# New priorities for the same tasks: one core, attention by hash buckets and two gated layers in one list schedule

## The chip, the cores and the metric

The kernel runs on one core of one Trainium2 chip. The metric is the device time of one execution in microseconds. The time before is 852.47 us, the median of three runs (852.0 to 852.72).

## What is computed

Three stages in float32, each feeding the next. First an attention over 2 batches of 8 heads, 768 rows of 64: six sign bits of `q @ proj` and `k @ proj` give each row a bucket, and a row attends only to rows of its own bucket. Then a gated layer on 1536 tokens, and then a second layer. The weights come as float64, in words of 64 bits.

```python
mask = q_bucket[:, :, :, None] == k_bucket[:, :, None, :]
scores = np.where(mask, scale * q @ k.T, -1e9)
attn = softmax(scores) @ v                      # 2 x 8 x 768 x 64
x = attn as 1536 x 512
xn = x / sqrt(mean(x * x) + 1e-6) * rms_g
x = (silu(xn @ w_gate) * (xn @ w_val)) @ w_out  # 512 -> 1536 -> 512
h = x @ w2_in                                   # 512 -> 2048
out = where(h > 0, h, exp(min(h, 0)) - 1) @ w2_out
```

## The kernel before

Each float32 factor is kept as two float32r parts, a rounded one (`hi`) and the remainder (`lo`), and a product is the sum of three matmuls. So nearly every tile that TensorE (PE) reads has been made by one copy on ScalarE (ACT), which rounds, and one subtraction on VectorE (DVE) or GpSimd (POOL), which forms the remainder.

The attention goes by 8 pairs of heads, and a pair by 6 units of 256 query rows. A unit is: scores of two blocks of 128 rows (`ps_s`, L477), their maximum on DVE (`nm`, L484), the exponential on ACT (`p`, L494), three turns of 4 transposes (`ps_p`, L522), the two parts of each turned tile (`pt`: ACT copy L530 and DVE subtraction L534; for some units the first turn goes through an ACT copy `pf`, L539, and two POOL instructions, L543 and L546), and three weighings of the values (`ps_v`, L569), which DVE joins into `ot` (L587). Beside the units the next pair is prepared: doubled rows `rd` on POOL, transposes `ps_t`, operands `tq` and `tk`, sign bits `ps_b` and counts `ps_c`. After a pair, its sums are inverted (`r`, L605 and L610), widened on POOL (`rw`, L618), transposed (`ps_x`, L627) and multiplied into `xT` (L636). After four pairs one batch is normalised: squares `sq`, `ps_z`, then multiplications (L731, L732) and a subtraction `xn` (L746), on POOL for the first batch and on DVE for the second.

The two layers go by 5 and 6 groups of hidden blocks of 128. A group's weights arrive in halves (`wraw`), and each half is converted: ACT L811, DVE L814, L820, L827 and L834 build float32 words from 64 bits (`wf`), ACT L855 rounds (`whi`), POOL L859 subtracts (`wlo`). A hidden block is `ps_h` (L908) on PE, then `sg`, `hf` and the two parts of `h` (L933 to L958); `ps_y` (L993) and `ps_o` (L1048) sum over a group, and DVE adds the sum up (L1005, L1060). The first group's blocks on the first batch begin while the last pair's attention still runs.

No engine's order is written out. Every task is handed to a planner (class `Plan`) with its engine, an assumed length, what it reads and writes, its buffers and a priority. The planner plays the program through: at each step it takes, over all engines, the task that can start first, and among tasks of one engine that could start at the same time the one with the smaller priority number. The instructions are then issued in that order, and on the chip each engine keeps to it and waits by semaphores.

A priority is a place in the natural order of units plus an offset from the table `OFF`, by kind of task and head pair: `S` scores, `max`, `exp`, `T` turns, `hi` and `lo` (and `plo` on POOL) the parts of `pt`, `V` weighings, `my` joins, `prep` and `post`, `norm` and `norm0` the normalisations, `ld` loads, `pv` values, `w0` and `w0s` the first group's weight loads, `wc` the conversions.

```python
fits.append(((t, prio), i))
plan.add("DVE", dve(S), top, [B_], [N_], prio + off("max", j))
prio += OFF["wc"]
```

Of the kernel before, what the change touches and what calls it, by code (L numbers as in the profile page):

```python
# [29 lines left out]
BYPOOL = ([0, 1, 2, 3, 4], [0, 2, 3, 4], [0, 1, 2, 3, 4, 5], [2, 4], [2, 4], [2, 4], [2, 4], [0])  # L30
HOT = ('DVE', 'ACT', 'ACT', 'DVE')
BW = (384, 512)
OFF = {'S': [-0.746, -0.843, -1.864, 66.85, -0.744, -0.758, -0.224, -0.41], 'max': [86.06, 128.957, 190.513, 53.124, 102.143, -5.035, -10.834, 24.749], 'exp': [119.567, 67.059, 76.291, 2.774, 75.069, 56.662, -35.846, 43.868], 'T': [0.573, 0.48, 0.307, 0.831, 0.703, 1.127, 1.259, 1.321], 'hi': [36.303, -33.663, 1.961, -57.136, 22.322, 57.959, -91.469, -121.974], 'lo': [-34.121, 9.653, 32.465, -109.77, -12.636, -87.223, -67.192, -11.818], 'V': [2.027, 1.953, 1.894, 2.015, 1.865, 2.222, 2.417, -11.303], 'my': [76.979, -114.216, -55.16, -8.134, -134.423, -45.978, -63.486, -29.752], 'ld': [16.116, 103.645, 134.666, -130.684, 51.199, 277.906, -45.786, 44.455], 'pv': [19.903, -68.605, 49.828, -156.296, 63.827, 116.499, -168.838, 19.653], 'prep': [-0.809, -2.78, -3.346, -0.341, -0.21, -0.194, 0.226, -82.459], 'post': [4.851, 4.774, 2.643, 1.592, 3.332, 9.244, 3.712, 28.29], 'plo': [-227.264, -10.728, 0.013, -54.307, -64.379, -36.39, 74.399, -48.961], 'wc': 0.693, 'ld1': 50.459, 'norm0': -125.474, 'rush': 27.318, 'pstep': 0.316, 'qstep': 0.146, 'norm': -8.853, 'w0': 189.461, 'w0s': 3.7229545865993564e+29}


class Plan:
# [143 lines left out]
def kernel(  # L180
# [69 lines left out]
    def off(key, j):  # L250
        return OFF[key][j]

# [12 lines left out]
    def dma(fn, nbytes, r=(), w=(), prio=None):  # L265
        return plan.add("SP", max(0.57, nbytes / 360e3), fn, r, w, prio, 2.7)
# [3 lines left out]
    def load_qk(j, prio, gate=()):  # L270
        b, h0 = divmod(2 * j, H)

        def go(i, a):
            if ("raw", j) not in st:
                st["raw", j] = slot([128, 2, 2, NC, D], F32, "raw")
            nc.sync.dma_start(
                out=st["raw", j][:, i, a], in_=(q, k)[i][b, h0 + a].rearrange("(p c) d -> p c d", c=NC)
            )

        for a in range(2):  # L280
            for i in range(2):
                dma(
                    lambda i=i, a=a: go(i, a), S * D * 4, r=[("go", j - 2), *gate],
                    w=[(("slot", "raw", j), i, a)], prio=prio + 0.05 * a,
                )
# [12 lines left out]
    def prep_v(j, prio):  # L298
        def hi(a):
            if ("vv", j) not in st:  # L300
                st["vv", j] = slot([128, 2, NC, 128], F32R, "vv")
            nc.gpsimd.tensor_copy(
                out=st["vv", j][:, a, :, 64 * a:64 * a + 64], in_=st["vn", j][:, a]
            )

        def lo(a):
            vv = st["vv", j]
            nc.gpsimd.tensor_tensor(
                out=vv[:, a, :, 64 - 64 * a:128 - 64 * a], in0=st["vn", j][:, a],
                in1=f(vv[:, a, :, 64 * a:64 * a + 64]), op=ALU.subtract,  # L310
            )

        for a in range(2):
            plan.add("Pool", 1.4, lambda a=a: hi(a), [("h3", "vn", j)], [(("slot", "vv", j), a, 0)], prio)
            plan.add(
                "Pool", 1.0, lambda a=a: lo(a),
                [("h3", "vn", j), (("slot", "vv", j), a, 0)], [(("slot", "vv", j), a, 1)], prio,
            )
# [124 lines left out]
    def prep(j, prio, step):  # L443
        p = prio
        for a in range(2):
            for i in range(2):
                twice(j, a, i, p)
                for hf in range(2):
                    prep_T(j, a, i, hf, p)
                    p += step  # L450
        for hf in range(2):
            prep_bits(j, hf, p)
            p += step
        for i in range(2):
            for hf in range(2):
                prep_count(j, i, hf, p)
                p += step
# [321 lines left out]
    def weights(g, m, part, prio, gate):  # L779
# [19 lines left out]
        dma(load, 128 * cols * (8 if wide else 4), r=gate, w=[R_], prio=prio)  # L799
        prio += OFF["wc"]  # L800
        if wide:
# [370 lines left out]
    prep_v(0, -15)  # L1172
    load_qk(1, OFF["ld1"])

    UPP = NC
    NU = NPAIR * UPP
    for j in range(NPAIR):
# [14 lines left out]
        if j + 1 < NPAIR:  # L1192
            prep(j + 1, base + off("prep", j), OFF["pstep"])
        hurry = OFF["rush"] if j == NPAIR - 1 else 0.0
        post(j, base + UPP + off("post", j) - hurry, OFF["qstep"])
        if j % PPB == PPB - 1:
# [70 lines left out]
```

## Time and profile before

| | us |
|---|---|
| median of three runs | 852.47 |
| the profiled execution | 852.93 |
| its span, first to last instruction | 851.1 |
| PE busy | 832.4 (98%) |
| DVE busy | 638.5 (75%) |
| ACT busy | 444.9 (52%) |
| POOL busy | 273.3 (32%) |

The profile is one execution. Busy time is the time in which an engine has at least one instruction in work; PE's matmuls overlap each other, so a busy PE is not PE at its peak. The shares are means over the whole span, and the stages differ: the attention fills roughly the first 290 us, the layers the rest. A wait in the lists is idle time of an engine together with the instruction whose end released it.

### The profile page before, as it was taken

Reading aid. Unit: us, or ns where it says so; the run is one execution under the profiler, and the core shown is the slowest. Engines: PE = TensorE matmul, PEld = TensorE weight load, DVE = VectorE, ACT = ScalarE, POOL = GpSimd, SP = SyncE. Lnnn points to the kernel's source line nnn. Section 1 sums busy time; section 2 is a strip of 40 time slices with the busy share of each in tenths; the row PEclk is TensorE's granted clock in tenths of the full one; section 3 lists DMA queues with packets and bytes.
Section 4 is the critical chain, followed back from the end, with each engine's and each line's share of the span. In section 5 each row is a group of like instructions: output and inputs, shape, how many; then the busy total and the mean of one; then the engine's idle time right before and its main releaser. Section 6 shows DMA issues by size and latency. Waiting matters only on the chain.

```text
span 851.1 us, 12464 instructions
## 1 busy us (share of the span) xinstructions
PE 832.4 (98%) x4722; PEld 736.7 (87%) x4722; DVE 638.5 (75%) x1015; ACT 444.9 (52%) x838; POOL 273.3 (32%) x289
## 2 busy tenths in 40 slices
PE   8999999998999999999999999999999999999998
PEld 7999999887998899999889898887888888888786
DVE  6999899999999987534364565579857778676754
ACT  6988988898987664432222322235444333332321
POOL 7857476789824312111011111110201101111100
PEclk9999999999999999999999999999999999999999
DMA  5102012330002200310111312213121302001003
GB/s 168 41 17 75 2 38 75 121 122 1 20 1 75 75 13 26 112 50 1 56 48 46 100 50 100 75 33 128 62 75 37 112 25 75 25 30 46 1 12 137
DMA packets 25708, 49.05 MB, mean 58 GB/s; under 512 B 2480, under 2 KB 8880, under 8 KB 25648
## 3 DMA queue, kind: packets, MB, share of 16 engines
q1 hardware_dynamic: 25648, 48.25, 17.3%
q8 instruction: 37, 0.61, 0.3%
q14 instruction: 23, 0.19, 0.1%
HBM read 45.09 MB, written 3.15 MB: 57 GB/s over the span
## 4 chain that ended last, share of the span: by engine, by line
PE 81%; DVE 13%; ACT 4%; issue 1%; POOL 1%; ACTq 0%; DVEq 0%; POOLq 0%
PE ps_h L908 37%; PE ps_o L1048 14%; PE ps_y L993 11%; PE ps_p L522 5%; PE ps_v L569 5%; PE ps_s L477 4%; DVE nm L484 3%; DVE pt L534 3%; PE ps_t L350 2%; PE ps_b L398 2%; ACT p L494 1%; ACT pt L530 1%; DVE wf L827 1%; DVE wf L834 1%; PE ps_w L1153 1%
## 5 line engine op out<-in xcount | busy, mean ns | idle before, releaser
L859 POOL TENSOR_TENSOR wlo<-wf,whi 128x768 fp32r<-128x768 f32 (+1 forms) x54 | 86.8, 1607 | 442.9 <-ACT whi L855 430.6
L908 PE MATMUL ps_h<-xn,whi 128*128 128x512 f32 (+2 forms) x768 | 190.2, 337 | 0.8 <-DVE hf L939 0.7
L908 PEld LDWEIGHTS ps_h<-xn,whi 128*128 128x128 f32 x768 | 133.5, 189 | 13.2 <-DVE hf L939 1.1
L908 PE MATMUL ps_h<-xn,wlo 128*128 128x256 f32 (+2 forms) x384 | 128.9, 336 | 0.0
L1048 PE MATMUL ps_o<-whi,h 128*128 128x512 f32 (+1 forms) x388 | 118.7, 387 | 0.8 <-DVE oa L1060 0.8
L908 PE MATMUL ps_h<-y,whi 128*128 128x512 f32 x384 | 118.2, 389 | 0.0
L933 ACT ACTIVATE sg<-ps_h 128x512 f32<-128x512 f32 (+1 forms) x87 | 50.7, 583 | 116.6 <-PE ps_h L908 114.5
L855 ACT CAST whi<-wf 128x768 fp32r<-128x768 f32 (+1 forms) x54 | 39.6, 733 | 118.2 <-DVE wf L834 118.2
L569 PE MATMUL ps_v<-pt,vv 128*128 128x256 f32 x576 | 96.8, 295 | 4.1 <-DVE pt L534 3.2
L954 ACT CAST h<-hf 128x512 fp32r<-128x512 f32 (+1 forms) x87 | 51.6, 605 | 88.1 <-DVE hf L939 49.1
L993 PE MATMUL ps_y<-h,whi 128*128 128x512 f32 (+1 forms) x312 | 91.4, 374 | 1.5 <-DVE ya L1005 1.5
L484 DVE TENSOR_REDUCE nm<-ps_s 128x1 f32<-128x768 f32 x96 | 90.6, 945 | 1.6 <-PE ps_s L477 0.9
L958 DVE TENSOR_TENSOR h<-hf,h 128x512 fp32r<-128x512 f32 (+1 forms) x87 | 71.0, 831 | 26.9 <-ACT h L954 26.2
L494 ACT ACTIVATE p<-ps_s,nm 128x768 f32<-128x768 f32 x96 | 87.2, 909 | 5.5 <-DVE nm L484 4.4
L522 PE MATMUL ps_p<-ident,p 128*128 128x128 f32 x576 | 86.0, 275 | 3.3 <-DVE pt L534 1.5
L477 PE MATMUL ps_s<-tk,tq 128*128 128x384 f32 x384 | 87.9, 350 | 0.6 <-ACT tk L428 0.4
L1048 PEld LDWEIGHTS ps_o<-whi,h 128*128 128x128 f32 x388 | 72.2, 188 | 16.4 <-DVE oa L1060 1.9
L569 PEld LDWEIGHTS ps_v<-pt,vv 128*128 128x128 f32 x576 | 79.3, 189 | 7.2 <-DVE pt L534 5.1
L908 PEld LDWEIGHTS ps_h<-y,whi 128*128 128x128 f32 x384 | 72.1, 188 | 15.0
L939 DVE TENSOR_TENSOR hf<-ps_h,sg 128x512 f32<-128x512 f32 (+1 forms) x39 | 25.2, 647 | 78.5 <-PE ps_h L908 78.5
L534 DVE TENSOR_TENSOR pt<-ps_p,pt 128x512 fp32r<-128x512 f32 x120 | 79.9, 680 | 2.7 <-ACT pt L530 1.8
L908 PEld LDWEIGHTS ps_h<-xn,wlo 128*128 128x128 f32 x384 | 72.6, 189 | 5.5
(111 smaller groups left out, 1501.0 us busy)
## 6 DMA issues: line engine op xcount, KB each, us to landing
wraw<-in_moe_w_out_dram SPq DMA_DIRECT2D x12, 768.0 KB, 4.9
wraw<-in_moe_w_in_dram SPq DMA_DIRECT2D x8, 768.0 KB, 4.6
wraw<-in_moe_w_out_dram SPq DMA_DIRECT2D x10, 512.0 KB, 4.1
raw<-in_q_dram SPq DMA_DIRECT2D x16, 192.0 KB, 3.4
raw<-in_k_dram SPq DMA_DIRECT2D x16, 192.0 KB, 3.7
vn<-in_v_dram SPq DMA_DIRECT2D x8, 384.0 KB, 3.3
wraw<-in_moe_w_gate_dram SPq DMA_DIRECT2D x4, 768.0 KB, 4.4
wraw<-in_moe_w_val_dram SPq DMA_DIRECT2D x4, 768.0 KB, 4.6
```

The costliest lines, as they stand in the source:

```text
L477: nc.tensor.matmul(st[B_][:, hf, 0:HS], lhsT=tq[:, x, c * 128:(c + 1) * 128], rhs=tk[:, x, hf * HS:(hf + 1) * HS], start=(x == 0), stop=(x ...
L484: nc.vector.tensor_reduce(out=st["nm", u, cc], in_=st[B_][:, :, 0:HS], axis=AX.XY, op=ALU.max, negate=True,)
L494: nc.scalar.activation(out=halves(st["p", u][:, cc]), in_=st.pop(B_)[:, :, 0:HS], func=AF.Exp, bias=st["nm", u, cc], scale=1.0, accum_out= ...
L522: nc.tensor.transpose(out=st[B_][:, o:o + 128], in_=p[:, cc, (2 * n + kt) * 128:(2 * n + kt + 1) * 128], identity=ident,)
L534: nc.vector.tensor_tensor(out=pt[:, 1], in0=st.pop(B_), in1=f(pt[:, 0]), op=ALU.subtract)
L569: nc.tensor.matmul(st[B_][:, 0:256], lhsT=st["vv", j][:, a, 2 * n + kt, :], rhs=pt[:, x, kt * 256:(kt + 1) * 256], start=(n == seq[0] and ...
L859: nc.gpsimd.tensor_tensor(out=l, in0=s["w"], in1=f(h), op=ALU.subtract)
L908: nc.tensor.matmul(ps[:, o:o + ln], lhsT=w[wp][:, kk, ft * 128:(ft + 1) * 128], rhs=t[xp][:, s:s + ln], start=(kk == 0 and n == 0), stop=( ...
L954: nc.scalar.copy(out=st["h", g, blk, ft][:, 0, 0:bw], in_=s["hf"])
L958: nc.vector.tensor_tensor(out=h[:, 1, 0:bw], in0=s["hf"], in1=f(h[:, 0, 0:bw]), op=ALU.subtract)
L993: nc.tensor.matmul(s["ps"][:, 0:bw], lhsT=wo[wp][:, ft, m * 128:(m + 1) * 128], rhs=h[:, xp, 0:bw], start=(ft == 0 and i == 0), stop=(ft = ...
L1048: nc.tensor.matmul(s["ps"], lhsT=h[:, xp, t * 128:(t + 1) * 128], rhs=wo[wp][:, ft, ds], start=(ft == 0 and i == 0), stop=(ft == n - 1 and ...
```

## The change

One line is replaced, the table `OFF`: all of its offsets but one (`pstep`) get new values. They were searched in a replay of the tasks in which every task carries the delay that was recorded for it on the chip. Tasks, engines, lengths, buffers and pools are as before. A part of the table's line, wrapped:

```diff
-OFF = {'S': [-0.746, -0.843, -1.864, 66.85, -0.744, -0.758, -0.224, -0.41],
-       'max': [86.06, 128.957, 190.513, 53.124, 102.143, -5.035, -10.834, 24.749],
+OFF = {'S': [-0.553, -0.871, -1.9, 118.401, -0.767, -0.421, -1.871, -0.924],
+       'max': [218.086, 185.37, 254.698, 115.887, 140.647, -73.551, -80.166, 37.818],
...
```

What follows from it is another order on four engines. In the printed order, where equal neighbours stand as one row, PE's queue has 856 lines of difference (of 2,554 rows before), DVE's 1,228 (of 922 rows, so nearly everything from the first difference on is shifted), ACT's 765, POOL's 236. The DMA queue on SP is the same.

On POOL, in the normalisation of the first batch: `xn` rows are the subtractions that wait for an ACT copy, `xT` rows the multiplications (by `y`, then by `gsc`). Before:

```order
L731 TENSOR_TENSOR xT_1927<-xT_1927,y_2440 128x384
L732 TENSOR_TENSOR xT_1927<-xT_1927,gsc_86 128x384
L746 TENSOR_TENSOR xn_2641<-xT_1221,xn_2641 128x384
L746 TENSOR_TENSOR xn_2686<-xT_1927,xn_2686 128x384
L731 TENSOR_TENSOR xT_1927<-xT_1927,y_2440 128x384
L732 TENSOR_TENSOR xT_1927<-xT_1927,gsc_86 128x384
```

And now, at the same place (the numbers in the names are the program's own and differ between the two):

```order
L731 TENSOR_TENSOR xT_1927<-xT_1927,y_2440 128x384
L732 TENSOR_TENSOR xT_1927<-xT_1927,gsc_86 128x384
L746 TENSOR_TENSOR xn_2653<-xT_1066,xn_2653 128x384
L731 TENSOR_TENSOR xT_1927<-xT_1927,y_2440 128x384
L732 TENSOR_TENSOR xT_1927<-xT_1927,gsc_86 128x384
L746 TENSOR_TENSOR xn_2688<-xT_1927,xn_2688 128x384
```

The second subtraction has moved behind the next block's two multiplications; the same swap is made once more for the other half of the columns.

On DVE, in the second unit of the sixth pair, while the first weight half is converted (`wf_2730` before, `wf_2786` now; `pt` rows are subtractions of turned tiles, `nm` maxima, `ot` a join). Before:

```order
L534 TENSOR_TENSOR pt_2843<-ps_p_2823,pt_2843 128x512
L827 SCALAR_TENSOR_TENSOR wf_2730<-wraw_2589,wf_2730 128x768
L484 TENSOR_REDUCE nm_2873<-ps_s_2846 128x1
L834 SCALAR_TENSOR_TENSOR wf_2730<-wraw_2589,wf_2730 128x768
L534 TENSOR_TENSOR pt_2881<-ps_p_2854,pt_2881 128x512
L534 TENSOR_TENSOR pt_2886<-ps_p_2862,pt_2886 128x512
L587 TENSOR_TENSOR ot_2884<-ps_v_2832,ot_2884 64x256
```

And now:

```order
L534 TENSOR_TENSOR pt_2842<-ps_p_2820,pt_2842 128x512
L484 TENSOR_REDUCE nm_2865<-ps_s_2830 128x1
L827 SCALAR_TENSOR_TENSOR wf_2786<-wraw_2590,wf_2786 128x768
L587 TENSOR_TENSOR ot_2876<-ps_v_2837,ot_2876 64x256
L534 TENSOR_TENSOR pt_2883<-ps_p_2854,pt_2883 128x512
L534 TENSOR_TENSOR pt_2886<-ps_p_2868,pt_2886 128x512
L484 TENSOR_REDUCE nm_2903<-ps_s_2878 128x1
L834 SCALAR_TENSOR_TENSOR wf_2786<-wraw_2590,wf_2786 128x768
```

The second conversion (L834) has moved behind both subtractions, and the join in front of them.

On DVE, at the end of the attention, in front of the last unit's subtractions (three `pt` rows). `wf_3132` before and `wf_3189` now is the last half of the first weight group, `wf_4043` before and `wf_4016` now the first half of the second group; `hf` and `h` belong to the first hidden block. Before:

```order
L827 SCALAR_TENSOR_TENSOR wf_3132<-wraw_2817,wf_3132 128x768
L587 TENSOR_TENSOR ot_3757<-ps_v_4003,ot_3757 64x256
L939 TENSOR_TENSOR hf_4059<-ps_h_4022,sg_3940 128x384
L814 TENSOR_SCALAR wf_4043<-wf_4043 128x768
L834 SCALAR_TENSOR_TENSOR wf_3132<-wraw_2817,wf_3132 128x768
L534 TENSOR_TENSOR pt_4067<-ps_p_4045,pt_4067 128x512
L534 TENSOR_TENSOR pt_4084<-ps_p_4054,pt_4084 128x512
L534 TENSOR_TENSOR pt_4086<-ps_p_4061,pt_4086 128x512
L958 TENSOR_TENSOR h_4089<-hf_4059,h_4089 128x384
L939 TENSOR_TENSOR hf_4110<-ps_h_4070,sg_4019 128x384
L820 TENSOR_SCALAR wf_4043<-wf_4043 128x768
```

And now:

```order
L820 TENSOR_SCALAR wf_4016<-wf_4016 128x768
L605 TENSOR_SCALAR r_4053<-sums_3624 128x12
L958 TENSOR_TENSOR h_4036<-hf_4009,h_4036 128x384
L610 RECIPROCAL r_4053<-r_4053 128x12
L827 SCALAR_TENSOR_TENSOR wf_4016<-wraw_3933,wf_4016 128x768
L834 SCALAR_TENSOR_TENSOR wf_3189<-wraw_2817,wf_3189 128x768
L834 SCALAR_TENSOR_TENSOR wf_4016<-wraw_3933,wf_4016 128x768
L534 TENSOR_TENSOR pt_4072<-ps_p_4046,pt_4072 128x512
L534 TENSOR_TENSOR pt_4089<-ps_p_4056,pt_4089 128x512
L939 TENSOR_TENSOR hf_4106<-ps_h_4074,sg_4061 128x384
L534 TENSOR_TENSOR pt_4092<-ps_p_4064,pt_4092 128x512
```

L820, L827 and L834 of the second group's first half now stand in front of the three `pt` rows, and so do the hidden block's subtraction and the second block's product.

## Rows read from the trace of the kernel before

**Rows 1.** Busy time by stage: stretch, length, then each engine, clock, DMA share, GB/s.

```profile
0.00:20.00 20.00, 17.16 (x101) 15.52 (x102) 13.52 (x37) 13.34 (x25) 14.17 (x29) 1.00 0.56 178
20.00:180.00 160.00, 159.26 (x1168) 149.99 (x1167) 150.66 (x249) 141.50 (x304) 111.88 (x143) 1.00 0.19 60
180.00:220.00 40.00, 35.05 (x244) 30.98 (x243) 38.60 (x62) 36.70 (x76) 37.48 (x40) 1.00 0.08 26
220.00:300.00 80.00, 75.59 (x531) 71.70 (x530) 79.21 (x121) 62.04 (x121) 35.92 (x33) 1.00 0.13 43
300.00:851.00 551.00, 545.34 (x2686) 468.47 (x2684) 356.46 (x551) 191.31 (x315) 73.82 (x47) 1.00 0.17 57
```

The engines are PE, PE's weight loads, DVE, ACT and POOL, in this order.

**Rows 2.** PE's waits, 180 to 300 us: releaser, us in total, times, longest.

```profile
PE ps_v L569 <- DVE pt L534: 3.2, 4, 1.2
PE ps_p L522 <- DVE pt L534: 1.5, 1, 1.5
PE ps_v L569 <- POOL pt L546: 0.8, 1, 0.8
...
PE ps_b L398 <- ACT pf L539: 0.4, 1, 0.4
```

**Rows 3.** DVE in order of time, 192 to 197 us: start, length, instruction.

```profile
192.07 1.25 DVE L827 SCALAR_TENSOR_TENSOR wf<-wraw,wf 128x768 int32<-128x768 int32 x1
...
194.11 0.94 DVE L834 SCALAR_TENSOR_TENSOR wf<-wraw,wf 128x768 int32<-128x768 int32 x1
...
196.17 0.40 DVE L587 TENSOR_TENSOR ot<-ps_v,ot 64x256 f32<-64x256 f32 x1
```

**Rows 4.** PE in order of time, 195 to 201 us; in brackets idle time and releaser.

```profile
195.71 0.66 PE L522 MATMUL ps_p<-ident,p 128*128 128x128 f32 x4 [1.47 <-DVE pt L534]
...
200.43 0.50 PE L569 MATMUL ps_v<-pt,vv 128*128 128x256 f32 x2 [0.83 <-POOL pt L546]
```

**Rows 5.** POOL in order of time, 179 to 201 us.

```profile
179.94 1.01 POOL L746 TENSOR_TENSOR xn<-xT,xn 128x384 fp32r<-128x384 f32 x1 [1.04 <-ACT xn L739]
...
189.62 1.00 POOL L746 TENSOR_TENSOR xn<-xT,xn 128x384 fp32r<-128x384 f32 x1 [0.75 <-ACT xn L739]
...
198.20 2.17 POOL L546 TENSOR_TENSOR pt<-pf,pt 128x512 fp32r<-128x512 f32 x1
```

**Rows 6.** DVE in order of time, 244 to 275 us.

```profile
244.65 1.21 DVE L605 TENSOR_SCALAR r<-sums 128x12 f32<-128x12 f32 x1
...
256.05 1.85 DVE L814 TENSOR_SCALAR wf<-wf 128x768 f32<-128x768 f32 x1
...
274.01 1.48 DVE L834 SCALAR_TENSOR_TENSOR wf<-wraw,wf 128x768 int32<-128x768 int32 x1
```

**Rows 7.** DVE in order of time, 280 to 293 us.

```profile
280.19 0.95 DVE L827 SCALAR_TENSOR_TENSOR wf<-wraw,wf 128x768 int32<-128x768 int32 x1
281.05 0.55 DVE L820 TENSOR_SCALAR wf<-wf 128x768 int32<-128x768 int32 x1
281.52 0.16 DVE L605 TENSOR_SCALAR r<-sums 128x12 f32<-128x12 f32 x1
281.60 0.95 DVE L834 SCALAR_TENSOR_TENSOR wf<-wraw,wf 128x768 int32<-128x768 int32 x1
...
284.92 2.60 DVE L834 SCALAR_TENSOR_TENSOR wf<-wraw,wf 128x768 int32<-128x768 int32 x1
...
289.25 1.48 DVE L958 TENSOR_TENSOR h<-hf,h 128x384 fp32r<-128x384 f32 x1
...
292.62 0.56 DVE L958 TENSOR_TENSOR h<-hf,h 128x384 fp32r<-128x384 f32 x1
```

**Rows 8.** POOL in order of time, at 285 us.

```profile
284.79 1.92 POOL L859 TENSOR_TENSOR wlo<-wf,whi 128x768 fp32r<-128x768 f32 x1 [0.62 <-ACT whi L855]
```

**Rows 9.** PE in order of time, 288 to 292 us.

```profile
288.19 1.70 PE L569 MATMUL ps_v<-pt,vv 128*128 128x256 f32 x12 [1.23 <-DVE pt L534]
...
291.25 0.62 PE L908 MATMUL ps_h<-xn,whi 128*128 128x384 f32 x2 [0.71 <-DVE hf L939]
```

More of the change, by code (lines that the diff above doesn't have):

```diff
@@ L32 @@
 BW = (384, 512)
-OFF = {'S': [-0.746, -0.843, -1.864, 66.85, -0.744, -0.758, -0.224, -0.41], 'max': [86.06, 128.957, 190.513, 53.124, 102.143, -5.035, -10.834, 24.749], 'exp': [119.567, 67.059, 76.291, 2.774, 75.069, 56.662, -35.846, 43.868], 'T': [0.573, 0.48, 0.307, 0.831, 0.703, 1.127, 1.259, 1.321], 'hi': [36.303, -33.663, 1.961, -57.136, 22.322, 57.959, -91.469, -121.974], 'lo': [-34.121, 9.653, 32.465, -109.77, -12.636, -87.223, -67.192, -11.818], 'V': [2.027, 1.953, 1.894, 2.015, 1.865, 2.222, 2.417, -11.303], 'my': [76.979, -114.216, -55.16, -8.134, -134.423, -45.978, -63.486, -29.752], 'ld': [16.116, 103.645, 134.666, -130.684, 51.199, 277.906, -45.786, 44.455], 'pv': [19.903, -68.605, 49.828, -156.296, 63.827, 116.499, -168.838, 19.653], 'prep': [-0.809, -2.78, -3.346, -0.341, -0.21, -0.194, 0.226, -82.459], 'post': [4.851, 4.774, 2.643, 1.592, 3.332, 9.244, 3.712, 28.29], 'plo': [-227.264, -10.728, 0.013, -54.307, -64.379, -36.39, 74.399, -48.961], 'wc': 0.693, 'ld1': 50.459, 'norm0': -125.474, 'rush': 27.318, 'pstep': 0.316, 'qstep': 0.146, 'norm': -8.853, 'w0': 189.461, 'w0s': 3.7229545865993564e+29}
+OFF = {'S': [-0.553, -0.871, -1.9, 118.401, -0.767, -0.421, -1.871, -0.924], 'max': [218.086, 185.37, 254.698, 115.887, 140.647, -73.551, -80.166, 37.818], 'exp': [222.396, 151.071, 131.687, 14.553, 167.978, 72.319, 8.908, 30.526], 'T': [0.617, 0.403, 0.208, 0.683, 0.724, 1.16, 0.704, 0.368], 'hi': [-5.439, -108.124, -104.303, -97.649, -1.792, -11.588, -0.478, -328.242], 'lo': [-25.885, 152.325, 50.654, -249.852, -94.55, -100.867, -94.047, 1.726], 'V': [2.023, 1.779, 1.845, 1.998, 1.765, 2.172, 2.091, -131.484], 'my': [86.252, -109.54, -86.917, 71.86, -211.471, -128.314, 3.301, -50.118], 'ld': [12.99, -9.023, 193.654, -326.658, 18.118, 419.853, -94.779, -2.721], 'pv': [13.348, -91.225, 113.233, -137.3, 139.674, 205.51, -230.333, 58.648], 'prep': [-0.609, -2.775, -3.408, -0.209, -0.168, -2.146, 0.85, -131.169], 'post': [3.076, 4.679, 2.352, 1.399, 3.331, 2.69, 3.463, -6.484], 'plo': [-339.354, -52.821, -82.568, -200.226, -58.483, -61.262, 272.84, -24.704], 'wc': -3.125, 'ld1': 77.433, 'norm0': -71.865, 'rush': 71.435, 'pstep': 0.316, 'qstep': 0.206, 'norm': 16.601, 'w0': 302.976, 'w0s': 1.5313431597767035e+52}
 class Plan:
```

## The prediction

> **What bounds the kernel now.** I read the table of busy time by stage first [rows 1]. TensorE (PE) is at the full clock in every stage, so the clock is not the question. From 300 us to the end PE is busy 545.34 of 551 us: that stage is PE's own work. From 20 to 180 us PE is busy 159.26 of 160, so at most 0.74 us is to be had there, although VectorE (DVE) is at 150.66 as well. The exception lies between 180 and 300 us, where the attention of the last three head pairs overlaps with the conversion of the first expert weights: PE idles 40 - 35.05 = 4.95 us and 80 - 75.59 = 4.41 us, together 9.4 us, while DVE is busy 38.60 of 40 and 79.21 of 80. In that stage DVE is what PE waits for, with GpSimd (POOL) beside it up to 220 us (37.48 of 40).
>
> Next the list of PE's waits in that stage [rows 2]: most end with DVE's subtraction of a turned probability tile (`pt`, L534), one with POOL's version of the same (L546), one with an ACT copy. Then the order of time, place by place. At 195.71 PE waits 1.47 us for `pt` [rows 4], because DVE stands at two weight conversions, 1.25 and 0.94 us, in front of it [rows 3]. At 200.43 PE waits 0.83 us for POOL's subtraction, which began at 198.20 and took 2.17 us; POOL itself had stood idle 1.04 and 0.75 us for an ACT copy [rows 5]. Between 244 and 291 us five DVE instructions take far longer than their like: 1.21 for an addition that takes 0.16 elsewhere, 1.85 where the same shape takes 0.55, 1.48 and 2.60 where it takes 0.95, 1.48 where it takes 0.56 [rows 6, 7]. The 2.60 one began 0.13 us after a POOL subtraction that ran to 286.71 [rows 8]; 2.60 less 0.95 is about the time for which POOL still ran. So these are waits of DVE for POOL, 1.05 + 1.30 + 0.53 + 1.65 + 0.92 = 5.45 us in all. PE sees the last ones as 1.23 us before the last `ps_v` and 0.71 us before the `ps_h` at 291.25 [rows 9]. I call that 291.25 the handoff: from it on PE runs almost without a gap to the end, so whatever moves the handoff moves the end by as much.
>
> **The change part by part.** No instruction is added or taken away, and the DMA queue on SP has the same order in both programs, so loads move only if the tasks that release them move. From 300 us on the order is nearly the same (a few neighbours on DVE and ACT change places, and one pair on PE, with the same set of instructions before each wait that the trace shows there). I cost that at nothing: PE has work throughout, and if that cover went, it would cost the length of a swapped neighbour, at most the 0.95 us of a conversion [rows 7]. The swaps before 180 us I cost at nothing too, bounded by the 0.74 us of PE idle time on the gain side and about as much on the other.
>
> First place, POOL at 180 to 190 us. A normalisation multiply now goes in front of each of the two subtractions that waited for ACT. The 1.04 and 0.75 us [rows 5] then have work under them, so POOL's queue is up to 1.79 us earlier when it comes to the `pt` that PE waits for at 200.43. The 0.83 us go.
>
> Second place, DVE at 192 to 196 us. The second conversion (0.94) moves behind both `pt` subtractions; a join (0.40) takes its place in front. PE's 1.47 us shrink by 0.94 - 0.40 = 0.54. With the 0.83, and the 0.4 that PE waits for ACT's `pf` copy [rows 2], which leaves earlier because PE's own turn leaves earlier, PE could be 0.54 + 0.83 + 0.4 = 1.8 us ahead by 207 us, just what POOL's 1.79 us allow. But DVE must be ahead as well if that is to last, since from 220 us on it has 0.79 us of idle time in 80. Between 180 and 220 it idles 1.40. So I count 1.4 us, not 1.8. Bounds: nothing, and 1.40 + 0.79 = 2.2.
>
> Third place, the end of attention. Three conversions of the second weight group (lengths 0.55, 0.95, 0.95 by [rows 7], from start to start 0.47 + 0.86 + 0.86 = 2.2 us) now stand in front of the last three `pt` subtractions; before, they stood behind the handoff, where PE did not need them. A subtraction and a product of the first hidden blocks also move in front of those, but they were ahead of the handoff already. So DVE has 2.2 us more to do before the handoff: 2.2 us lost, whatever is done to the order, unless DVE has idle time there, which the table does not show.
>
> Against that stand the 5.45 us in which DVE waits for POOL. The new order moves every one of the five in DVE's queue: the addition 4 places earlier, the 1.85 one 11 earlier, the conversion of 1.48 by 21 earlier, the one of 2.60 by 3 later, the hidden block's subtraction 4 earlier; and the POOL subtractions that follow from them move too. What the trace does not show is who meets whom then. The upper bound is that all five meetings go (5.45). The lower bound is that all come back and one more like the longest is added (-1.65). The stage has as many conversions and as many POOL subtractions as before plus three conversions, and only 45% of POOL's time is busy from 220 us on [rows 1], so a meeting is about an even chance for each; the last one in front of the handoff looks likely, since the first hidden subtraction now follows a conversion whose POOL half is then due. I take half, 2.7 us.
>
> The page SBUF — State Buffer of the Trainium skill, in Who interferes with whom, says that a VectorE instruction with two SBUF inputs contends with a GpSimd one that reads SBUF, and that the one issued first holds the shared port for its whole length. The pair at 284.79 and 284.92 agrees. By that rule such a delay belongs to the meeting of two instructions and not to the task that recorded it, so priorities found with the delay tied to the task would place it wrongly; with no gain from meetings the sum would be 1.4 - 2.2, a loss of 0.8 us.
>
> The sum: 1.4 + 2.7 - 2.2 = 1.9 us off the profiled execution, which took 852.93 (851.1 in the span and 1.8 around it). That is 851.0. The median of the three runs is 852.47, 0.46 lower, so I forecast 850.6 for the median.
>
> **The rivals.** (A) The meetings of DVE and POOL come back in other pairs: gain 1.4, loss 2.2, so 0.8 us slower, 853.3. For it: POOL's subtraction of each weight half follows its own conversion by one ACT copy of under 1 us in either order, and DVE then usually has the next conversion in hand. Against it: the costliest meeting rests on a 0.13 us difference in start [rows 7, 8].
> (B) Slower, by one mechanism: the three conversions in front of the last `pt` subtractions. The last `ps_v` waits for DVE already (1.23 us, [rows 9]). If DVE comes to these subtractions later than PE has turned the last tile, each conversion in front adds its whole length to that wait, and what PE won before 207 us is lost in the same queue, because DVE was full all the way. Price 2.2 us: 854.7. It decides from the point at which DVE has no idle time left in front of the last turned tile; before, it had 0.79 us of it in the whole of the 80 us [rows 1].
> (C) A larger gain: DVE's idle time from 180 to 300 us (2.2) and all five meetings (5.45) go, less 2.2: 5.4 us faster, 847.0. For it: PE idles 9.4 us there, so there is room. Against it: all terms at their best ends at once.
> (D) The change does nothing. The printed order of PE's queue differs in 856 lines, against some 2,550 rows in all, so this one is out.
>
> **How the numbers follow.** Forecast (0.7 to 3.2 us faster, its own range 849.3 to 851.8): 0.44. (A) 0.22, (B) 0.20, (C) 0.14. About 0.2% of the time, 1.7 us, is what a measurement can tell from no change. The forecast's centre lies only 0.2 us beyond that, so of its 0.44 I put 0.27 to faster and 0.17 to no change; (C) adds 0.14 and a little more from between the two goes to faster. (A) goes to no change for 0.17, the rest to slower with most of (B). Faster 0.43, same 0.35, slower 0.22. The range that should hold 8 of 10 goes most of the way to (C) and to (B): 847.6 to 854.3.
>
> **What would show it.** POOL's two waits for the ACT copy at 180 to 190 us are gone, and PE's wait for POOL's `pt` with them; PE is busy some 1.5 to 2 us more between 180 and 220 us. DVE instructions at over 1.2 us of the conversion lines between 220 and 300 us sum to about half of the 5.45 us. The last `ps_v` group still waits about 1 us for DVE. The first `ps_h` behind the last turned tile of the last pair starts near 289.3 instead of 291.25, and from there to the end the length is the same to 0.3 us. Wrong would be: a handoff at or after 291; meetings of DVE and POOL at as many places as before; or a changed length from the handoff to the end, which would say that the few swaps there matter.

## The result, and the profile of the changed kernel

The changed kernel is slower: 857.3 us (median of 4 runs, 856.65 to 857.41) against 852.54 for the kernel before beside it, a ratio of 1.0055 with a 95% interval of 1.0043 to 1.0067. The forecast was 850.6 in a range of 847.6 to 854.3, so the sign was wrong, and the time lies 3.0 us above the upper end.

The table of busy time by stage (stretch, length, then PE, PE's weight loads, DVE, ACT and POOL, granted clock, DMA share, GB/s) answers [rows 1], here from 180 to 300 us:

```profile
180.00:220.00 40.00, 35.63 (x249) 31.72 (x248) 38.41 (x60) 36.19 (x73) 38.03 (x41) 1.00 0.18 60
220.00:300.00 80.00, 73.80 (x507) 68.97 (x507) 77.56 (x122) 62.15 (x120) 35.31 (x31) 0.98 0.12 41
```

PE is 0.6 us busier from 180 to 220 us, where 1.5 to 2 were forecast, and 1.8 us less busy from 220 to 300, where the clock is 0.98 instead of 1.00. DVE, which was to be full, idles more in both stretches: 1.59 us instead of 1.40, and 2.44 instead of 0.79. The list of PE's waits from 180 to 300 us (releaser, us in total, times, longest) answers [rows 2]:

```profile
PE ps_v L569 <- DVE pt L534: 2.4, 2, 1.9
PE ps_p L522 <- DVE ot L587: 1.8, 2, 1.0
PE ps_h L908 <- ACT sg L933: 1.1, 1, 1.1
PE ps_c L419 <- ACT pf L539: 1.1, 1, 1.1
```

The wait for POOL's `pt` is gone, as forecast. The waits of `ps_v` for DVE's `pt` are fewer, but the longest has grown from 1.2 to 1.9 us, and two new waits of 1.1 us have come, both for ACT instructions that empty a bank for PE's next result (the activation `sg` and the copy `pf`). The longest is the one in front of the last weighing. PE in order of time there, with idle time and releaser in brackets, answers [rows 9]:

```profile
291.50 1.22 PE L569 MATMUL ps_v<-pt,vv 128*128 128x256 f32 x8 [1.89 <-DVE pt L534]
292.56 1.31 PE L627 MATMUL ps_x<-ident,rw 128*128 128x128 f32 x6
293.52 1.20 PE L569 MATMUL ps_v<-pt,vv 128*128 128x256 f32 x4
294.52 0.84 PE L908 MATMUL ps_h<-xn,whi 128*128 128x384 f32 x2
```

The handoff has moved from 291.25 to 294.52 us, 3.27 later, where 289.3 was forecast. DVE in front of it answers [rows 7], and POOL [rows 8]:

```profile
284.77 0.56 DVE L820 TENSOR_SCALAR wf<-wf 128x768 int32<-128x768 int32 x1
...
285.93 2.43 DVE L827 SCALAR_TENSOR_TENSOR wf<-wraw,wf 128x768 int32<-128x768 int32 x1
288.28 2.44 DVE L834 SCALAR_TENSOR_TENSOR wf<-wraw,wf 128x768 int32<-128x768 int32 x2
290.75 1.29 DVE L534 TENSOR_TENSOR pt<-ps_p,pt 128x512 fp32r<-128x512 f32 x2
```

```profile
285.48 2.06 POOL L859 TENSOR_TENSOR wlo<-wf,whi 128x768 fp32r<-128x768 f32 x1 [11.67 <-ACT whi L855]
287.49 1.55 POOL L618 COPY rw<-r 128x768 f32<-128x768 f32 x1
```

The three hoisted conversions are all there: L820, L827 and the second of the two L834. L827, 0.95 us alone, took 2.43 because POOL's subtraction had begun 0.45 us earlier; the two L834 behind it met POOL's subtraction no longer but its widening copy (the pair took 2.44 where two in a row take 0.86 + 0.95 = 1.81). PE's last turn had ended at 286.15, and ACT's copies of the turned tiles began at 287.10; DVE came to the first `pt` at 290.75.

The span is 855.5 us instead of 851.1, and that splits into three parts. The handoff is 3.27 later. From there to the start of the last matmul it is 556.07 us against 556.04 (850.59 less 294.52, 847.29 less 291.25). From that start to the end of the span it is 4.91 us against 3.81, 1.10 more. The sum is 4.40.

### The profile page after: what moved, and what is told of

Read it like the earlier page. It is cut to its first block, busy times and chain, and to the rows that moved or that the text cites. A ratio compares the mean times of both kernels' runs of the same rounds, so it can differ in the third digit from the quotient of the medians.

```text
span 855.5 us, 12458 instructions
## 1 busy us (share of the span) xinstructions
PE 834.4 (98%) x4722; PEld 737.4 (86%) x4722; DVE 637.7 (75%) x1015; ACT 445.8 (52%) x838; POOL 273.5 (32%) x289
## 4 chain that ended last, share of the span: by engine, by line
PE 78%; DVE 15%; ACT 4%; issue 2%; POOL 1%; DVEq 0%; ACTq 0%; POOLq 0%
PE ps_h L908 36%; PE ps_o L1048 14%; PE ps_y L993 11%; PE ps_v L569 4%; PE ps_p L522 4%; PE ps_s L477 4%; DVE nm L484 4%; DVE pt L534 3%; PE ps_t L350 2%; PE ps_b L398 1%; DVE wf L827 1%; ACT pt L530 1%; DVE ot L587 1%; ACT p L494 1%; DVE wf L820 1%
## 5 line engine op out<-in xcount | busy, mean ns | idle before, releaser
L569 PE MATMUL ps_v<-pt,vv 128*128 128x256 f32 x576 | 94.7, 294 | 2.5 <-DVE pt L534 2.4
L958 DVE TENSOR_TENSOR h<-hf,h 128x512 fp32r<-128x512 f32 (+1 forms) x87 | 67.8, 792 | 26.8 <-ACT h L954 26.1
```

What stands on the lines that cost most here:

```text
L569: nc.tensor.matmul(st[B_][:, 0:256], lhsT=st["vv", j][:, a, 2 * n + kt, :], rhs=pt[:, x, kt * 256:(kt + 1) * 256], start=(n == seq[0] and ...
L958: nc.vector.tensor_tensor(out=h[:, 1, 0:bw], in0=s["hf"], in1=f(h[:, 0, 0:bw]), op=ALU.subtract)
```

## The experiments

All kernels but the last one carry both tables. The planner runs once with each, and the order that is issued is spliced: pieces of one order or the other, each up to a named task, and then some tasks moved behind another one. The numbers in the edits are those of the tasks, in the order in which they are handed to the planner. Nothing else is changed. Where an edit has no `PIECES`, all of the order is the new one (three_back, six_back) or the old one (old_front and the runs behind it).

```diff
-        for i in self.order():
+        for i in spliced(self.order(0), self.order(1)):   # 0: old table, 1: new table
```

| run | us | before beside it | ratio, 95% interval |
|---|---|---|---|
| changed kernel | 857.30 | 852.54 | 1.0055 (1.0043 to 1.0067) |
| new_to_224 | 857.12 | 852.64 | 1.0053 (1.0039 to 1.0067) |
| new_224_to_275 | 855.02 | 852.64 | 1.0030 (1.0020 to 1.0040) |
| new_from_275 | 859.10 | 852.64 | 1.0077 (1.0065 to 1.0090) |
| three_back | 855.75 | 852.64 | 1.0047 (1.0034 to 1.0060) |
| new_to_206 | 852.91 | 852.28 | 1.0004 (0.9995 to 1.0013) |
| six_back | 853.13 | 852.28 | 1.0009 (1.0000 to 1.0018) |
| old_front | 856.89 | 852.28 | 1.0055 (1.0043 to 1.0068) |
| old_wo_late | 855.35 | 852.28 | 1.0033 (1.0020 to 1.0045) |
| front_no_meet | 855.90 | 852.31 | 1.0044 (1.0031 to 1.0056) |
| wo_first | 856.38 | 852.31 | 1.0045 (1.0032 to 1.0059) |
| six_later | 850.77 | 852.59 | 0.9979 (0.9969 to 0.9988) |

Theory E, from the traces: the loss is made at the end of the attention, by the conversions in front of the last subtractions. Its rival M: it is made from 225 to 275 us, where the last pair's preparation is late and DVE idles 0.68 us at 242 and 1.00 us at 247 behind ACT copies. A third, R: the early lead only brings DVE and POOL together in other pairs.

**Whole stretches of one order.**

```diff
+PIECES = [(1, 1355), (0, 1555), (0, None)]   # new_to_224: new up to the scores (39, 0)
+PIECES = [(0, 1355), (1, 1555), (0, None)]   # new_224_to_275; 1555: last weighing of unit 45
+PIECES = [(0, 1355), (0, 1555), (1, None)]   # new_from_275
```

> The order of the new table up to the scores of unit 39 (224 us in the trace of the changed kernel), from there the order of the old table for all tasks that are left. Theory E (the loss sits at the end of attention: three weight conversions in front of the last subtractions of turned tiles): the early lead of PE, 2 to 3 us at 212 to 230 us, is kept as far as DVE allows, so 850.5 to 851.5 against 852.5 before. Theory M (the loss sits between 225 and 275 us, where the seventh and eighth pair's preparation is late): the same, 850.5 to 851.5. Rival R (the lead only brings VectorE and GpSimd to meet in other pairs later): 852 to 854. No theory makes it slower than 854.

> Old order up to the scores of unit 39, the new order from there to the last weighing of unit 45 (about 275 us), then the old order again. Theory E: within 0.5 us of before, 852.0 to 853.0, since the end is the old one. Theory M (DVE idles 0.7 and 1.0 us at 241 and 247 us behind the late preparation of the last pair, and the scores of the last pair start 4 us later): 854.5 to 856.5, slower by 2 to 4 us. Rival R gives no sign.

> Old order up to the last weighing of unit 45 (about 275 us), the new order from there. Theory E: the three hoisted conversions (2.2 us) stand in front of the last subtractions, and one of them meets GpSimd's subtraction (2.43 us where it takes 0.95): 855.5 to 857, slower by 3 to 4.5 us. Theory M: at most 853.3, since half of the conversions' time is idle time of DVE that PE's lateness made.

These three misled more than they told. All came out slower, new_to_224 by 4.5 us where every theory had at most 1.5. The traces show why: at a cut where the two orders have done different tasks, those that one order had put off come all at once. In new_to_224 these are the last pair's transposes, and PE stands for 1.17, 0.79 and 0.52 us between 225 and 231 us; in new_from_275 six conversions stand in a row on DVE, from 273.20 to 279.25, in front of a join that a hidden block waits for, 3.19 us at 279.73. So the cuts made stalls that neither kernel has. What can be kept is little: new_224_to_275 has the new order's 1.10 us wait for `pf` at 245.79, so M is real in kind. Its time, 855.02, lies in the range that M had, but 1.04 us of PE's waits there are again for a join just behind the cut (279.26), so M's size isn't to be had from this run.

**Three conversions put back.**

```diff
+MOVES = [([1696, 1697, 1698], 1592), ([1699, 1700], 1708)]   # L820, L827, L834 behind the last pt
```

> The new order, with only the second group's first three VectorE conversions (L820, L827, L834 of its first half) moved back behind the last turned tile's subtraction, and the ScalarE and GpSimd halves of that weight moved back with them. Theory E: 853 to 854, that is 3 to 4.5 us below the changed kernel's 857.3 (2.2 us of conversions, about 1 us of the meeting, 0.65 us of the lower clock). Theory M: 855.5 to 856.5, since the last turned tile was late by 1.6 us before the conversions came. Under both the stretch of 3.4 us at half the granted clock behind 292 us may stay or go; it is worth 0.65 us.

The time is 1.55 us below the changed kernel's, a number that M had right and E not, but by luck, as the traces show. The handoff comes at 292.05, 2.5 us earlier, as E says, and PE and DVE show where the rest went. (The profiled execution, 858.1 us, is the longest of the five, 855.57 to 858.1, so the wait may be shorter in the others.)

```profile
303.82 2.76 PE L674 MATMUL ps_z<-sq,ones 128*128 128x384 f32 x4 [2.43 <-DVE sq L658]
```

```profile
296.12 2.15 DVE L827 SCALAR_TENSOR_TENSOR wf<-wraw,wf 128x768 int32<-128x768 int32 x1
...
301.45 2.31 DVE L658 TENSOR_TENSOR sq<-sq 128x768 f32<-128x768 f32 x1
```

The new order has the conversions of the weight's second half in front of the norm's squares; with the first three behind the handoff, six stood there, and the column sum `ps_z` waited. That gave the next edit.

**All six put back, and the early part by itself.**

```diff
+MOVES = [([1696, 1697, 1698], 1592), ([1699, 1700], 1708),   # six_back
+         ([1716, 1717, 1718], 1712), ([1719, 1720], 1608)]   # second half behind the squares
+PIECES = [(1, 1213), (0, None)]   # new_to_206: cut where the orders differ by one task
```

> The new order with the second group's three conversions (L820, L827, L834 of its first half) behind the last turned tile's subtraction, and, other than in the run three_back, those of its second half too behind the squares that the norm's column sum waits for (where the old order has them). Theory E (each conversion adds its length to the next wait of PE that stands behind it in VectorE's queue): the 2.43 us in front of ps_z at 303 us go, the handoff stays near 292.0, so 853.0 to 853.8. If the wait in front of ps_z was POOL's or ACT's and not the queue's: 855 to 856, as three_back.

> The new table's order up to the exponential of unit 35 (206 us in the changed kernel's trace), where the two orders have done the same tasks but one, then the old table's order. It holds the prediction's first and second place (POOL's and DVE's swaps) and nothing of what comes later. If the lead of PE at 207 us (about 1.1 us there) is kept to the handoff: 851.2 to 851.8. If VectorE, which is full from 220 us on, gives it all back: 852.3 to 852.9. A loss of over 0.7 us would say that the early part itself does harm.

six_back met E: 853.13, with the handoff at 291.45 and no wait in front of the last weighing.

PE in order of time, and then DVE:

```profile
289.37 1.11 PE L569 MATMUL ps_v<-pt,vv 128*128 128x256 f32 x8
...
291.45 0.51 PE L908 MATMUL ps_h<-xn,whi 128*128 128x384 f32 x2
```

```profile
287.64 1.29 DVE L534 TENSOR_TENSOR pt<-ps_p,pt 128x512 fp32r<-128x512 f32 x2 [1.34 <-ACT pt L530]
```

Without the conversions DVE has 1.34 us to spare in front of the last subtractions, where it waits for ACT's copy of the turned tile.

Everything else in the new table is a loss of 0 to 1.5 us in sum (the interval); the rest goes with the six conversions: 3.07 us of the handoff, and 1.1 us behind the last matmul that only the changed kernel has (see the tail). That small sum has two large parts. In six_back only three DVE rows in front of the last subtractions are still stretched, at 226, 249 and 271 us as in the changed kernel, 1.9 us of the 5.45 [rows 6, 7], and PE's waits for DVE's `pt` from 220 us on are gone, 3.2 us. But PE's list from 220 to 315 us has others in their place:

```profile
PE ps_h L908 <- ACT sg L933: 1.7, 2, 1.1
PE ps_c L419 <- ACT pf L539: 1.1, 1, 1.1
PE ps_s L477 <- ACT p L494: 1.0, 3, 0.5
PE ps_t L350 <- DVE ot L587: 0.6, 1, 0.6
PE ps_c L419 <- DVE tq L430: 0.4, 1, 0.4
```

Up to the handoff (0.58 of the first row lies behind it) they come to 4.2 us, as much as PE waited before from 220 us on (3.2 for `pt`, 0.71 and 0.34). Some 2.9 of the 4.2 lie between 228 and 252 us, where M has its loss. So M is real, and it took back what the meetings gave; no run took these waits away one by one.

new_to_206 says of the early part: no change. The lead is spent at once, and the same five DVE rows are long as before [rows 6, 7], so R is not at work there. From 180 to 220 us PE is busier, but part of that is slower work, since the granted clock there is 0.96:

```profile
180.00:220.00 40.00, 36.65 (x248) 32.58 (x247) 38.74 (x61) 36.30 (x73) 36.65 (x39) 0.96 0.16 54
220.00:300.00 80.00, 75.65 (x530) 71.82 (x530) 79.17 (x120) 62.09 (x121) 36.13 (x33) 1.00 0.13 44
```

From 220 to 300 us it shows the same busy times as before to 0.06 us on PE [rows 1], and the handoff is at 291.29.

**The hoist alone, in the old order.**

```diff
+MOVES = [([1696, 1697, 1698], 1684)]                         # old_front
+MOVES = [([1696, 1697, 1698], 1684), ([1685, 1686], 1705)]   # front_no_meet: whi, wlo later
```

> The old order with one edit: the second group's first three VectorE conversions (L820, L827, L834) in front of the last three subtractions of turned tiles, as the new table has them. Theory E (rival B of the prediction): each adds its whole length, 2.2 us, and a stretched one 0.5 to 1.5 more: 854.8 to 856.5. Rival: the conversions only take the place of idle time or of a meeting with POOL that goes: 852.3 to 853.4.

> As old_front (three conversions in front of the last subtractions of turned tiles, 856.9), and the ScalarE copy whi of the first group's last half moved behind the first hidden copy, so that GpSimd's subtraction that follows it no longer runs beside the last of the three conversions. Theory E: that conversion takes 0.95 us instead of 2.44 and the subtractions come 1.5 us earlier: 855.0 to 855.5; lower still, down to 854.5, if less of the stretch at half the granted clock is left. If the meeting costs nothing beyond the wait that is there anyway: 856.5 to 857.2.

Three rows moved in the old order cost 4.6 us (856.89 is 0.4 above E's upper end). With six_back, which takes the loss away from the new order, this is the run that settles it. (That the whole new table costs about as much is in part chance: there 3.27 us are the handoff and 1.10 the tail, here the handoff comes 4.03 us later, at 295.28, and the tail is 3.82, as before.) DVE and PE:

```profile
286.75 0.55 DVE L820 TENSOR_SCALAR wf<-wf 128x768 int32<-128x768 int32 x1
287.33 0.96 DVE L827 SCALAR_TENSOR_TENSOR wf<-wraw,wf 128x768 int32<-128x768 int32 x1
288.32 2.44 DVE L834 SCALAR_TENSOR_TENSOR wf<-wraw,wf 128x768 int32<-128x768 int32 x1
290.68 1.87 DVE L534 TENSOR_TENSOR pt<-ps_p,pt 128x512 fp32r<-128x512 f32 x3
```

```profile
291.42 2.93 PE L569 MATMUL ps_v<-pt,vv 128*128 128x256 f32 x12 [5.17 <-DVE pt L534]
```

From the first of them to the `pt` it is 3.93 us, and PE's wait grew by 3.94, from 1.23 [rows 9] to 5.17: nothing hid them. The weighing itself took 2.93 us instead of 1.70, since the granted clock fell to half during the wait (0.50 from 290 to 294 us). In front_no_meet POOL's `wlo` no longer ran beside the third conversion:

```profile
289.26 0.96 DVE L834 SCALAR_TENSOR_TENSOR wf<-wraw,wf 128x768 int32<-128x768 int32 x1
```

```profile
290.87 2.93 PE L569 MATMUL ps_v<-pt,vv 128*128 128x256 f32 x12 [3.68 <-DVE pt L534]
```

That conversion is 1.48 us shorter and PE's wait 1.49, as expected of the mechanism. The time fell by 1.0 us, to 0.4 above the upper end expected, and the intervals of the two ratios overlap, so the meeting's price is shown in the trace and not in the times. Of the 3.93 us, then, 2.4 are the conversions' own and 1.5 the meeting.

**Conversions taken out of the way.** If three conversions in front of the last subtractions cost that much, the conversions of [rows 7] that the old order has there should be worth something too. The last half of `wo` (L820, L827, L834 of the 2.60 us row) is not needed before `ps_y` at 309 us.

```diff
+MOVES = [([1682, 1683, 1684], 1606), ([1685, 1686], 1722)]   # old_wo_late: behind the norm's squares
+MOVES = [([1682, 1683, 1684], 1704), ([1685], 1705), ([1686], 1685),   # wo_first: behind hf
+         ([1696, 1697, 1698, 1716, 1717, 1718], 1638), ([1699, 1700, 1719, 1720], 1756)]
+MOVES = [([1682, 1683, 1684], 1704), ([1685], 1705), ([1686], 1685),   # six_later
+         ([1696, 1697, 1698], 1802), ([1699, 1700], 1804),
+         ([1716, 1717, 1718], 1806), ([1719, 1720], 1818)]
```

> The old order with one edit in the other direction: the three conversions (L820, L827, L834) of the first group's last half, which only the sum ps_y at 309 us needs, moved from in front of the last subtractions of turned tiles to behind the squares at 299.6 us, with their ScalarE and GpSimd halves. Theory E: the 2.60 us conversion no longer stands in front of the last subtractions, so PE's 1.23 us at the last ps_v and part of the 0.71 us at the handoff go: 850.8 to 851.6. Rival: ps_y then waits for the GpSimd half instead, or another conversion meets POOL in its place: 852.2 to 853.5.

> The old order with the first group's last conversions (L820, L827, L834 of the half that ps_y needs) behind the product of the second hidden block, so behind the handoff, as in old_wo_late but ahead of the norm; and the six conversions of the second group's first weight, which nothing needs before 340 us, moved behind the norm's last subtraction (318 us). Theory E: the handoff comes at 288.7 as in old_wo_late, no conversion stands in front of the z copies, and the 2.6 us are kept to the end: 849.4 to 850.2. If the norm's own chain, or wlo for ps_y, ends later than PE then needs it: 851 to 853.

> As wo_first, but the six conversions of the second group's first weight are not put in one block behind the norm (where they stood in front of two hidden blocks' products, 1.7 and 1.6 us of PE's time): three go behind the hidden block at 340 us and three behind the next, where the trace of before shows VectorE busy for only 1.67 of 10 us and the weight is not needed before 353 us. Theory E: handoff at 288.7 and nothing given back: 849.4 to 850.2, faster than both kernels. If something else takes the 2.6 us (a buffer that comes free later, so that a weight load or a copy waits; wlo too late for ps_h at 353 us): 851 to 855.

In old_wo_late the handoff came at 288.66, 2.6 us earlier, with no wait in front of the last weighing, and the kernel was 3.1 us slower all the same. The rival had the sign and one of its two causes in part: the moved conversions now stood in front of DVE's copies of the norm's sums, and the POOL subtraction that follows them met another conversion there, 2.60 us for 0.96. DVE, and PE's list from 220 to 315 us:

```profile
299.92 2.60 DVE L827 SCALAR_TENSOR_TENSOR wf<-wraw,wf 128x768 int32<-128x768 int32 x1
```

```profile
PE ps_h L908 <- DVE z L682: 3.4, 1, 3.4
```

wo_first put them in front of the norm instead, and six others, which are not urgent, in one block behind it. The handoff stayed early and nothing waited in the norm, but the block stood in front of one hidden block's product, and its two POOL subtractions ran beside the two `h` subtractions (3.29 us at 321.98, 1.02 in six_later) ahead of the other's:

```profile
319.53 0.62 PE L908 MATMUL ps_h<-xn,whi 128*128 128x384 f32 x2 [1.68 <-DVE hf L939]
```

The other wait is 1.55 us, at 327.59, with a third of 1.65 us at 334.72. After three_back and old_wo_late this is the third expectation of E missed in the same way: the conversions cost as much again in the place to which they were moved. six_later gave each group of three a place where DVE has idle time, and there they hide:

```profile
336.38 0.56 DVE L939 TENSOR_TENSOR hf<-ps_h,sg 128x384 f32<-128x384 f32 x1 [2.88 <-PE ps_h L908]
...
338.00 0.55 DVE L820 TENSOR_SCALAR wf<-wf 128x768 int32<-128x768 int32 x1
```

It is 850.77, faster than both kernels (0.9979, 0.9969 to 0.9988). That is 1.8 us below the kernel before, where E had 2.4 to 3.2. The handoff came at 288.06, 3.2 us earlier, and the span fell by 2.1 (849.0): a wait of 0.62 us for a join at 291.02 is new, and the time from the last matmul's start to the end is 4.20 us instead of 3.81.

**The tail.**

> The changed kernel itself once more, for its tail: in its profile 4.9 us lay between the start of the last matmul and the end of the span, in that of before 3.8. If that belongs to the order of the program it is 4.9 again; if it is how one store landed in one execution, about 3.8 and a span of 854.4. The handoff (first ps_h behind the last ps_x) is at 294.5 under both.

The second profile of the changed kernel has its last matmul's start 4.99 us before the end of the span (850.01, 855.0), so the longer tail belongs to this program. In the other twelve profiles it is 3.7 to 4.2. The lists of DMA queues at the end show one more load of instructions there than in six_back. The changed kernel, from 850 us on (packets, MB, share; then the issue with its size in KB and time to landing):

```profile
q14 instruction: 2, 0.02, 0.5%
...
out_dram<-oa SPq DMA_DIRECT2D x1, 128.0 KB, 3.1
```

And six_back from 847 us on:

```profile
q14 instruction: 1, 0.01, 0.5%
...
out_dram<-oa SPq DMA_DIRECT2D x1, 128.0 KB, 1.9
```

The last store takes 1.2 us longer to land. That the instruction load delays it is argued from these lines only; no run took it away.

## Why the prediction was wrong

**What bounds the kernel** was read rightly for the kernel before: DVE decides when the handoff comes (old_front, old_wo_late), and the handoff decides the last matmul, which starts 556.00 to 556.11 us behind it in the profiles of before, the changed kernel, six_back, new_to_206 and old_front. A changed length behind the handoff was named as a sign of being wrong, but for the swaps there; what changed, by 1.1 us, is the time after the last matmul. In the new order without the hoisted conversions DVE is no longer the only bound: PE then waits for ACT (six_back).

**The early gain** of 1.4 us did not come. Of the 1.79 us for which POOL waited for ACT [rows 5] half stayed, as its list of waits from 170 to 205 us shows:

```profile
POOL xn L746 <- ACT xn L739: 0.9, 2, 0.6
```

PE's wait for POOL's `pt` did go, and its wait at 195 us shrank from 1.47 to 1.03 (194.81), near the 0.54 that was counted. But new waits, 0.49 us for `rw` at 208.11 and 0.66 for a join at 210.40, took part of it back, and the step needed DVE to lose its idle time, while DVE idled 0.19 us more. new_to_206 shows that nothing of the early lead reaches the handoff.

**The hoisted conversions** were priced at their 2.2 us. In the new order they moved the handoff by 3.07 us (294.52 against 291.45 in six_back), in the old one PE's wait by 3.94. The place and the direction were right, the size was not. Against six_back DVE comes to the last subtractions 3.11 us later (290.75 against 287.64): about 2.3 of the conversions' own and 2.1 of meetings with POOL, less the 1.34 us of idle time that is used up first. PE's own work ahead of the weighing covers 0.98 of it. And from the weighing to the handoff PE takes 3.02 us instead of 2.08, 0.94 more, because its clock fell: a term that the prediction put at nothing ("so the clock is not the question").

**The failed step** is the gain set against them: "The upper bound is that all five meetings go... I take half, 2.7 us". It failed twice. Every microsecond that DVE no longer loses was counted as one of PE's. But in six_back more than half of the 5.45 us are gone and the handoff is at 291.45, not before 291.25: with the early gain, 4.1 us were forecast and -0.2 came, because PE's waits for ACT and for late preparation stand in the place of those for `pt`. And meetings were counted as a pool from which the new order draws by chance, apart from the conversions. In the changed kernel they are not apart. POOL's subtraction follows its conversion by one ACT copy, and with more conversions in front of the last subtractions two meetings came there, where they lengthen PE's wait; front_no_meet shows for the old order that such a meeting goes when that copy is moved. Up to the last subtractions the changed kernel has five stretched ones too, which answer [rows 6, 7]: the two at 285.93 and 288.28 above, 1.48 and 0.63 us too long, and these, whose length is 0.55 undisturbed, 0.90, 0.36 and 0.63 too long:

```profile
226.15 1.45 DVE L820 TENSOR_SCALAR wf<-wf 128x768 int32<-128x768 int32 x1
...
248.68 0.91 DVE L814 TENSOR_SCALAR wf<-wf 128x768 f32<-128x768 f32 x1
...
270.95 1.18 DVE L814 TENSOR_SCALAR wf<-wf 128x768 f32<-128x768 f32 x1
```

That is 4.0 us in all, so 1.4 went instead of 2.7, and the two nearest the end, 2.1 us, stand in the queue that PE waits for. (A sixth, 1.82 us for 0.55 at 293.02, lies behind the last subtraction, and PE waited for nothing behind it.)

By the Trainium skill (SBUF — State Buffer, Who interferes with whom) whichever of the two engines is issued first keeps the shared port for its whole instruction. The pair at 285.48 (POOL) and 285.93 (DVE) agrees, and the loss that the prediction worked out beside that rule, 0.8 us, had the right sign.

**The rivals.** (B), with a chance of 0.20, was what happened at the end of the attention: its place, its mechanism and its condition (no idle time of DVE left in front of the last turned tile), at 4.6 us in old_front and 3.3 us of the handoff in the changed kernel instead of 2.2. The other 1.1 us of the changed kernel are the tail, which no case had. (A) had the meetings returning, which they mostly did, but no more conversions' time than 2.2. (C) and "nothing changes" are out. Every case, (B) too, took 2.2 us for these three rows and no more; that is why the range ended at 854.3.

**What stays open:** which of PE's new waits in six_back could be had back, with the 0 to 1.5 us that it still lacks against the kernel before, and the tail.

## What to carry to other kernels

An engine that is nearly full just ahead of a handoff passes on every instruction that is put in front of it, at its stretched length and not its own; price such a move with the meeting that it brings, and subtract only idle time that the trace shows in that very place. Time that such an engine gains is not yet time that PE gains: look for the wait that ends next (in six_back PE's waits for DVE went, and as many for ACT and late preparation came). Work that has to wait must be given a stretch where its engine idles: moved in one block behind the handoff, conversions cost 3 to 4 us here, and only spread over DVE's gaps from 338 us on did they pay. Two orders spliced where they have not done the same tasks make stalls of their own, so move few named rows, or cut where the sets agree.

## What the runs showed of the hardware

PE's granted clock fell to half after idle times that looked harmless. In the changed kernel, behind PE's waits of 1.11 and 1.89 us (the column behind POOL is the granted clock):

```profile
291.00:293.00 2.00, 1.50 (x11) 1.50 (x12) 2.00 (x4) 1.79 (x3) 2.00 (x2) 0.93 0.01 4
293.00:295.00 2.00, 2.00 (x11) 2.00 (x10) 2.00 (x3) 0.37 (x2) 1.43 (x1) 0.50 0.03 8
```

The hidden block's first two matmuls take 0.64 us from start to start of the next (294.52 to 295.16), where two take 0.35 in six_back (291.45 to 291.80). In new_to_206 the same happened at 211 us behind waits of only 0.49, 0.33 and 0.16 us, while before passed through waits of 1.47 and 0.83 us [rows 4] at the full clock, and six_back through the same 1.11 us at 287.18. What decides it these runs do not show. In old_front the 5.17 us wait left the clock at half through all twelve weighings, 1.23 us on top of the wait itself.
